# Strided attention and a gated layer on one core: 32 short filler matmuls for one of 352 columns, and a step list derived anew

## The chip, the core and the metric

The kernel runs on one core of one Trainium2 chip. The metric is the time of one execution on the device in microseconds (us), less is better; the median of several executions counts. The engines of the core work in parallel, each in its own program order: TensorE (PE, with its weight loads as PEld), VectorE (DVE), ScalarE (ACT), GpSimd (POOL) and SyncE (SP), which here issues all DMAs.

## The reference

Eight batches of eight heads with 576 positions of 64 go through attention with a mask: the first four heads see the 32 latest positions, the other four see the positions of the same residue modulo 32. The 4608 rows of 512 that come out go through a gated layer.

```python
scores = scale * np.matmul(q, k.transpose(0, 1, 3, 2))
mask_local = (rel >= 0) & (rel < stride)
mask_strided = (rel >= 0) & (pos[None, :] % stride == pos[:, None] % stride)
scores = np.where(masks[None, :, :, :], scores, -1000000000.0)
attn = np.exp(scores - max); attn = attn / (sum(attn) + 1e-09)
x = (attn @ v).transpose(0, 2, 1, 3).reshape(4608, 512)
...
gate = 1.0 / (1.0 + np.exp(-(x @ w_gate)))
out = (gate * (x @ w_val)) @ w_out
```

## The kernel before

**The work.** Attention is cut into pieces. A piece is two pairs of heads of one batch (a local one with 10 slots, 128 x 640 scores, or a strided one with 12 slots, 128 x 648). The first eight pieces (batches 0 and 1) have step names that begin with f; the others are numbered 0 to 23. Each goes through the same steps: LQ loads queries and keys, S makes the scores on PE, M adds the mask and A takes the row maximum on DVE, U subtracts it, E takes the exponential on ACT, N sums and inverts the row on DVE, W scales, B.0 to B.3 transpose 32 x 32 blocks on DVE (line 537), X multiplies with the values on PE, H and L split the result in two parts, R keeps the last columns. A score or value step is 20 to 44 small matmuls on quarters or eighths of the array.

**The gated layer.** Rows are taken in blocks of 512 (k from 0). Every operand is split into a high and a low part, so a product is three matmuls of 128x512 for each 128 of the depth. Blocks 0, 1 and 2 are done plainly: g and v (12 matmuls each), s, m, x and y on ACT and DVE, o or oh on PE. Blocks 3 to 8 are done two at a time with a seven-product scheme: G and V (lines 986, six matmuls each) make half products, c, ad, sg and mu combine them, ta to td form differences, hx and hy split the hidden values, Oa and Ob (line 1065, three matmuls each) multiply them with the output weights, ok, oa and os give out. Their weight sets are made by the kernel (steps pa, pb, ph, pw, pd), stored to device memory and read back into a ring of slots (step r).

**The order.** All of it stands in one list by hand or by an outside planner, the text ORDER. A word is a step and its numbers. The loop at the end of the kernel calls the steps in the order of the list, and every engine gets its instructions in that order; nothing is moved afterwards. A letter v or p behind a step's name (pbv, hyp, tdv, xlp) says that DVE or POOL does it in place of the usual engine.

**Fillers.** The step J issues matmuls of a constant tile whose result nobody reads. J0 makes the tile; J576, J352, J1024, J1088 and J256 (twice) stand among the first scores. They are F32 products, and the trace shows each F32 matmul as two records.

```python
    def busy(n):
        ...
        for at in range(0, n, BANK):
            m = min(BANK, n - at)
            nc.tensor.matmul(o[:, :m], ones[:, :P], ones[:, :m], start=True, stop=True)
```

The first scores (fSa0.0 and fS0.0, tiles sa and s, line 425) wait for the first load of queries and keys.

Of the kernel before, what the change touches and what calls it, by code (L numbers as in the profile page):

```python
# [96 lines left out]
wl3.1 wb4.1 wd4.1 wa5.0 ws5.0 wl3.2 wlp3.0 fg3.0 s0.3 fV1.1 wb5.1 fM1.1 y0.2 wlp2.2 wa4.2 ws4.2 wb4.2 wdp5.0 wb6.0 wu5.0 wu4.1 fg3.1 m0.3 wr6.1 x0.3
fg4.0 wl4.1 y0.3 wl5.0 wdp4.2 wr7.1 wa5.1 ws5.1 wd5.1 o0.2 wa6.0 ws6.0 wd6.0 wu4.2 wlp4.2 fg4.1 s0.4 wb6.1 wu5.1 fg5.0 wlp5.1 wu6.0 wb5.2 wr7.0 wa6.1
m0.4 x0.4 o0.3 wlp6.0 wa7.0 pl2 wb7.0 ws6.1 wd6.1 wa5.2 fg5.1 wb7.1 ws7.0 wu6.1 wd7.0 wlp6.1 ws5.2 wd5.2 s0.5 fg6.0 wu5.2 wa7.1 wl5.2 ws7.1 wd7.1 y0.4
m0.5 wu7.0 wu7.1 wa6.2 ws6.2 wb6.2 wd6.2 fg6.1 x0.5 y0.5 wlp7.1 wr8.1 wa8.1 wr7.2 s0.6 wl7.0 fg7.0 wu6.2 wl6.2 wb8.1 wb7.2 m0.6 wr8.0 wa8.0 wb8.0  # L100
ws8.0 wd8.0 wa7.2 ws7.2 wd7.2 fg7.1 fA1.1 wr8.2 fU1.1 s0.7 wu8.0 wl8.0 wr9.0 o0.4 x0.6 o0.5 wu7.2 wl7.2 y0.6 o0.6 fE1.1 ws8.1 wd8.1 wa8.2 ws8.2 fN1.1
fg8.0 wb8.2 wdp8.2 wr9.1 fWp1.1 fY1.1 wu8.1 wlp8.1 wa9.0 wb9.0 wu8.2 m0.7 fg8.1 ws9.0 wlp8.2 wr9.2 wd9.0 x0.7 wu9.0 wa9.1 fB1.1.0 fB1.1.1 fB1.1.2
wb9.1 wl9.0 wa9.2 fQ1.2 fS1.2 ws9.1 wd9.1 wr10.0 ws9.2 wb9.2 wdp9.2 wr10.1 wu9.1 y0.7 fB1.1.3 s0.8 m0.8 wa10.0 wb10.0 wu9.2 fg9.0 wlp9.1 ws10.0
wdp10.0 fg9.1 wr10.2 fM1.2 fA1.2 wb10.1 fU1.2 wa10.1 wu10.0 ws10.1 s0.9 wlp10.0 o0.7 fE1.2 fQ1.3 wlp9.2 x0.8 wa10.2 wb10.2 fX1.1 wr11.0 fV1.2 wd10.1
wu10.1 fg10.0 fn1.2 fH1.1 wr11.1 fR1.1 y0.8 ws10.2 fN1.2 fW1.2 fY1.2 wlp10.1 fB1.2.0 wdp10.2 m0.9 fg10.1 wb11.0 wa11.0 fL1.1 fS1.3 s0.10 ws11.0
wdp11.0 wu11.0 wlp11.0 wu10.2 wb11.1 wa11.1 o0.8 fg11.0 wr11.2 x0.9 pl4 fB1.2.3 fB1.2.1 fB1.2.2 fZ1.3 fM1.3 fX1.2 fV1.3 fA1.3 fU1.3 fE1.3 y0.9 m0.10
o0.9 wlp10.2 ws11.1 wdp11.1 LQ0 wu11.1 fH1.2 fR1.2 wb11.2 pl0 fN1.3 fW1.3 fY1.3 fB1.3.0 fB1.3.1 fB1.3.2 s0.11 wlp11.1 fg11.1 fB1.3.3 fL1.2 fX1.3 x0.10
y0.10 fH1.3 fL1.3 fR1.3 o0.10 pl1 g1.0 m0.11 wa11.2 ws11.2 wd11.2 x0.11 wu11.2 wl11.2 y0.11 pav0.0.0 v1.0 s1.0 m1.0 oh0.11.1 S0.0 M0.0 M0.1 oh0.11.0
pl3 A0 U0 e0.0 x1.0 y1.0 e0.1 g1.1 E0 N0 v1.1 pbv0.0.0 s1.1 g1.2 m1.1 x1.1 LQ1 LV0 v1.2 D0 y1.1 W0 d0.1 e0.3 d0.0 e0.2 Y0 B0.1 d0.3 B0.3 B0.2 o1.0
d0.2 s1.2 m1.2 S1.0 LQ2 B0.0 X0.0 po4 Z1 LV1 pa0.0.1 Y1 pb0.0.1 M1.0 M1.1 ph0.0.0.1 pwp0.0.0 pd0.0.0 R0 g1.3 v1.3 A1 U1 x1.2 y1.2 pa0.1.0 pb0.1.0 o1.1  # L110
E1 ph0.0.1.0 N1 W1 s1.3 B1.0 pw0.0.1 m1.3 x1.3 y1.3 D1 g1.4 v1.4 s1.4 g1.5 pd0.0.1 ph0.1.0.1 pav0.1.1 pbv0.1.1 ph0.1.1.0 m1.4 v1.5 pwp0.1.1 x1.4 y1.4
s1.5 pw0.1.0 o1.2 H0 L0 B1.2 B1.1 B1.3 X1.0 R1 pd0.1.1 pav1.0.1 m1.5 S2.0 M2.0 pd0.1.0 pa1.0.0 pbv1.0.0 M2.1 LQ3 A2 pbv1.0.1 ph1.0.1.0 pw1.0.1 pd1.0.1
U2 o1.3 pa1.1.1 g1.6 ph1.0.0.1 pw1.0.0 pd1.0.0 pa1.1.0 pb1.1.0 v1.6 Y2 o1.4 x1.5 y1.5 o1.5 s1.6 E2 N2 pbv1.1.1 ph1.1.1.0 pwp1.1.1 pd1.1.1 m1.6 x1.6
y1.6 ph1.1.0.1 pw1.1.0 g1.7 s1.7 H1 W2 B2.2 v1.7 m1.7 x1.7 pd1.1.0 LV2 pa2.0.0 g1.8 v1.8 o1.6 pb2.0.0 y1.7 s1.8 B2.0 L1 B2.1 B2.3 X2.0 m1.8 D2 R2 S3.0
Z3 pav2.0.1 pbv2.0.1 ph2.0.1.0 pwp2.0.1 o1.7 ph2.0.0.1 pwp2.0.0 M3.0 M3.1 po1 A3 v1.9 D3 x1.8 g1.9 LQ4 pd2.0.1 H2 Y3 U3 E3 N3 W3 pav2.1.1 y1.8 s1.9
B3.0 o1.8 B3.2 g1.10 m1.9 x1.9 LV3 y1.9 pbv2.1.1 ph2.1.1.0 pw2.1.1 B3.1 L2 pd2.0.0 B3.3 pa2.1.0 pb2.1.0 ph2.1.0.1 pwp2.1.0 s1.10 v1.10 m1.10 x1.10
# [111 lines left out]
def attention_then_glu(ctx, tc, qk_l, qk_s, v_l, v_s, w_all, consts, out, out_t):  # L228
    nc = tc.nc
# [867 lines left out]
    def by_gpsimd(step):  # L1097
# [133 lines left out]
```

## Time and profile before

| | |
|---|---|
| median of three runs | 901.21 us (899.53 to 901.92) |
| the profiled execution | 898.98 us, span 897.2 us |
| around the span | 1.78 us |
| PE busy | 889.0 us, 99% of the span |
| DVE, ACT, POOL busy | 628.8, 477.8, 327.8 us |
| instructions | 17941, of them 7050 matmuls |

The span runs from the first to the last instruction of the profiled execution. Busy times are the sum over an engine of the time in which it had an instruction. The chain that ended last is followed back from the last instruction, at each step to what released it; it tells on which engine the time was spent.

### The profile page before, as it was taken

To read this page: it belongs to the slowest core of one execution; us is meant where nothing else is said; L and a number is where in the kernel's file an instruction comes from. 1 tells how busy PE (TensorE), PEld (TensorE's weight loads), DVE (VectorE), ACT (ScalarE), POOL (GpSimd) and SP (SyncE) were. 2 spreads that over 40 slices of the span, in tenths; PEclk is the share of its full clock that TensorE was granted. 3 is DMA by queue.
4 is the path that set the end of the run, shared out by engine and by line. 5 is a ranking of instruction groups with operands and counts; after the bars stand their busy time and mean duration, and the time that the engine had idled before them with its cause. 6 is when DMAs were issued, how large, how long until landed. Compare 5 with 4: busy or idle time off the path is not lost.

```text
span 897.2 us, 17941 instructions
## 1 busy us (share of the span) xinstructions
PE 889.0 (99%) x7050; PEld 726.1 (81%) x7050; DVE 628.8 (70%) x1025; ACT 477.8 (53%) x869; POOL 327.8 (37%) x392
## 2 busy tenths in 40 slices
PE   8999999999999999999999999999999999999998
PEld 5788888888887788888878888888888888888886
DVE  6888877677778887889998976556667723433553
ACT  5888765443445554576564654344455623423453
POOL 4452631434663544675633420100132300221362
PEclk9999999999999999999999999999999999999999
DMA  9864685553573667898878758666655667655664
GB/s 349 331 229 138 217 280 168 165 163 109 158 247 99 178 182 267 245 323 288 252 249 274 258 181 271 219 205 198 216 180 194 214 192 232 195 176 204 235 205 148
DMA packets 116869, 193.63 MB, mean 216 GB/s; under 512 B 7600, under 2 KB 58800, under 8 KB 116784
## 3 DMA queue, kind: packets, MB, share of 16 engines
q1 hardware_dynamic: 116784, 192.47, 65.3%
q8 instruction: 56, 0.92, 0.4%
q14 instruction: 29, 0.24, 0.1%
HBM read 149.98 MB, written 42.47 MB: 214 GB/s over the span
## 4 chain that ended last, share of the span: by engine, by line
PE 89%; DVE 7%; ACT 2%; DMA 1%; issue 1%; SPq 0%; DVEq 0%; ACTq 0%
PE p L986 21%; PE oc L1065 19%; PE d L986 15%; PE o L713 10%; PE g L682 9%; PE v L682 9%; PE s L425 1%; PE x L603 1%; DVE pt L537 1%; PE gv L682 1%; PE x L575 1%; PE s_g L425 1%; DMA qk<-in_qk_l 1%; DVE sb L474 1%; ACT sb L489 1%
## 5 line engine op out<-in xcount | busy, mean ns | idle before, releaser
L986 PE MATMUL p<-xs,ring 128*128 128x512 f32 x864 | 210.9, 391 | 0.1
L986 PEld LDWEIGHTS p<-xs,ring 128*128 128x128 f32 x864 | 161.3, 188 | 34.2 <-issue 0.5
L986 PE MATMUL d<-xs,ring 128*128 128x512 f32 x648 | 160.0, 390 | 0.2 <-DVE hid L1013 0.2
L986 PEld LDWEIGHTS d<-xs,ring 128*128 128x128 f32 x648 | 121.2, 188 | 26.4 <-DVE hid L1013 0.9
L1065 PE MATMUL oc<-hh,ring 128*128 128x512 f32 x312 | 103.8, 389 | 0.0
L713 PE MATMUL o<-w,hh 128*128 128x512 f32 x288 | 90.5, 395 | 0.0
L1013 DVE TENSOR_TENSOR e<-e,d 128x512 f32<-128x512 f32 x54 | 37.0, 684 | 72.6 <-PE d L986 55.6
L682 PE MATMUL g<-xh,w 128*128 128x512 f32 x256 | 85.8, 393 | 0.8 <-DVE sb L449 0.5
L682 PE MATMUL v<-xh,w 128*128 128x512 f32 x256 | 85.0, 390 | 0.0
L1036 POOL TENSOR_TENSOR hid<-hid,hid 128x512 f32<-128x512 f32 x23 | 31.0, 1351 | 113.5 <-DVE hid L1030 87.8
L1065 PE MATMUL oc<-ops,ring 128*128 128x512 f32 x288 | 72.3, 389 | 0.0
L1050 ACT CAST hh<-hid 128x512 fp32r<-128x512 f32 x78 | 46.7, 620 | 42.9 <-PE oc L1065 31.5
L1065 PEld LDWEIGHTS oc<-hh,ring 128*128 128x128 f32 x312 | 58.6, 188 | 12.2
L1008 ACT COPY e<-p 128x512 f32<-128x512 f32 x54 | 31.7, 587 | 66.9 <-PE p L986 57.1
L1013 DVE TENSOR_TENSOR hid<-hid,d 128x512 f32<-128x512 f32 x54 | 36.8, 681 | 39.5 <-PE d L986 21.9
L898 POOL TENSOR_TENSOR sum<-w 128x256 f32<-128x256 f32 x49 | 39.4, 823 | 67.3 <-DMA sets<-sum 43.6
L1065 PEld LDWEIGHTS oc<-ops,ring 128*128 128x128 f32 x288 | 54.0, 188 | 11.3
L713 PEld LDWEIGHTS o<-w,hh 128*128 128x128 f32 x288 | 53.0, 188 | 11.4
L1008 ACT COPY hid<-p 128x512 f32<-128x512 f32 x54 | 31.7, 588 | 54.5 <-PE p L986 54.3
L1065 PE MATMUL oc<-hl,ring 128*128 128x512 f32 x156 | 60.7, 389 | 0.0
L903 POOL TENSOR_TENSOR sum<-sum 128x128 f32<-128x128 f32 x100 | 53.3, 534 | 18.8 <-DVE sum L898 5.5
L537 DVE STREAM_TRANSPOSE pt<-sb 32x320 f32<-32x320 f32 (+1 forms) x112 | 55.4, 495 | 3.3 <-POOL pt L376 1.0
(178 smaller groups left out, 1717.8 us busy)
## 6 DMA issues: line engine op xcount, KB each, us to landing
ring<-sets SPq DMA_DIRECT2D x126, 512.0 KB, 4.9
ring<-osets SPq DMA_DIRECT2D x63, 512.0 KB, 4.5
raw<-in_w_all SPq DMA_DIRECT2D x36, 512.0 KB, 5.7
qk<-in_qk_l SPq DMA_DIRECT2D x14, 608.0 KB, 5.0
qk<-in_qk_s SPq DMA_DIRECT2D x14, 594.0 KB, 5.4
sets<-w SPq DMA_DIRECT2D x24, 256.0 KB, 4.6
sets<-sumh SPq DMA_DIRECT2D x24, 256.0 KB, 2.9
sets<-sum SPq DMA_DIRECT2D x24, 256.0 KB, 3.1
```

The lines of the kernel that those rows point to most:

```text
L425: nc.tensor.matmul(sc[j % len(sc)][g * m : (g + 1) * m, j // len(sc) * BANK + (s - lo) * kk : j // len(sc) * BANK + (s - lo + 1) * kk], q[ ...
L537: nc.vector.transpose(dst[band * LB : (band + 1) * LB, at : at + n, col * LB : (col + 1) * LB], src[part * LB : (part + 1) * LB, x : x + n ...
L682: nc.tensor.matmul(o, w, x, start=first and n == 0, stop=last and n == len(todo) - 1)
L713: nc.tensor.matmul(acc[k][i], h[:, i * P : (i + 1) * P], w, start=f == 0 and n == 0, stop=f == NF - 1 and n == 2,)
L898: by.tensor_tensor(to, part(wh[f][i], c), part(wl[f][i], c), op=ALU.add)
L903: by.tensor_tensor(u[:, to], u[:, x], u[:, y], op=op)
L986: nc.tensor.matmul(to, w[:, (wi * 2 + c) * P : (wi * 2 + c + 1) * P], x[xi][:, c], start=p in (1, 2, 5) and c == j == 0, stop=c == 1 and j ...
L1008: nc.scalar.copy(x, two[m, 0])
L1013: nc.vector.tensor_tensor(x, x, two[m, 1], op=ALU.add)
L1036: by.tensor_tensor(h[to], h[x], h[y], op=ALU.subtract)
L1050: nc.scalar.copy(ops[q, p][0], hidden_tile(k, q, KEPT[str(p)]))
L1065: nc.tensor.matmul(chains[m, at], w[:, (wi * 2 + m) * P : (wi * 2 + m + 1) * P], x[xi], start=p in (1, 2, 5) and q == j == 0, stop=q == PA ...
```

## The change

The step J352 becomes Jt32: 32 matmuls of 32 columns with 32 columns of weights, all of the same constant tile and to the same place. From its eighth line on the list has its steps in a new order; they are the same steps, but 74 of them are given to the other one of DVE and POOL (among them sum parts pb, differences ta to td, low parts hy and xl). The values of piece 20 (X20.1) and the scores of piece 21 (S21.1) stand behind each other in it.

```diff
-fQb0.0 fZ0.0 fZ0.1 J0 K fZ0.3 fZ0.2 fQa0.0 fQa0.1 fQb0.1 wr2.0 fQ0.2 wr1.0 fQ0.3 C J576 fK0.1 wr0.0 fV0.1 fKa0.0 fV0.0 fK0.0 fV0.2 J352 fSa0.0 fV0.3
+fQb0.0 fZ0.0 fZ0.1 J0 K fZ0.3 fZ0.2 fQa0.0 fQa0.1 fQb0.1 wr2.0 fQ0.2 wr1.0 fQ0.3 C J576 fK0.1 wr0.0 fV0.1 fKa0.0 fV0.0 fK0.0 fV0.2 Jt32 fSa0.0 fV0.3
...
+    def busy_short(n):
+        ones, o = busy_with
+        for _ in range(n):
+            nc.tensor.matmul(o[:32, :32], ones[:, :32], ones[:, :32], start=True, stop=True)
+
...
     STEPS = dict(
-        J=busy,
+        J=busy, Jt=busy_short,
...
-Oa3.4.4 Ob3.4.4 B20.2 Oa3.5.4 Ob3.5.4 r57 S21.1 os3.1.7 ok3.0.4 ok3.1.4 V5.0.1 G5.0.1 r58 c5.0.1.1 oa3.0.3 G5.0.2 os3.0.3 c5.0.0.1 os3.1.4 V5.0.6
-c5.0.1.6 ad5.0.0.2 V5.0.2 G5.0.6 r59 ad5.0.1.2 V5.0.5 sg5.0.2 mu5.0.2 G5.0.5 c5.0.0.6 B20.1 hx5.0.1 B20.3 Z21 M21.0 R19 xh5.1.3 xlp5.1.3 M21.1 A21
-G5.0.7 c5.0.0.7 ad5.0.0.7 U21 V5.0.7 c5.0.1.7 G5.0.4 ad5.0.1.7 V5.0.4 r60 sg5.0.7 mu5.0.7 E21 sg5.0.4 X20.1 os3.0.7 H20 Y21 N21 V5.0.3 G5.0.3 LQ22 r63
...
+hyp3.4.4 Ob3.4.4 Oa3.4.4 r54 B20.2 R19 Ob3.5.4 B20.1 B20.3 X20.1 S21.1 LQ22 Oa3.5.4 ok3.1.4 V5.0.1 ok3.0.4 G5.0.1 c5.0.0.1 r56 V5.0.2 oa3.0.3 G5.0.2
```

On PE, at the program's beginning, unread is the fillers' place, s and sa are the first scores; this is one piece of the difference:

```order
 L412 LDWEIGHTS cst
 L412 MATMUL s_0_130<-cst 128x128
-L802 MATMUL unread<-ones 128x352
+L807 MATMUL unread<-ones 32x32 x32
 L425 MATMUL sa_0_125<-qk_0_80 32x64 x24
 L425 MATMUL s_0_130<-qk_0_80 32x64 x12
 L425 MATMUL s_1_118<-qk_1_100 64x54 x22
```

The filler keeps its place, between the last mask products and the first scores, which stand behind it in PE's queue.

On PE, between the last output products of blocks 3 and 4 (oc3) and the first half products of blocks 5 and 6 (p15), the scores of piece 21 (s21) stood alone before:

```order
L1065 MATMUL oc3_1_1_5994<-hh3_5_4_6535,ring52_6460 128x512
L1065 MATMUL oc3_1_1_5994<-hl3_5_4_6536,ring52_6460 128x512
L1065 MATMUL oc3_1_1_5994<-hh3_5_4_6535,ring52_6460 128x512
L425 MATMUL s21_6571<-qk7_1_6245 64x54 x24
L986 MATMUL p15_0_6601<-xs5_1_0_5834,ring53_6508 128x512
```

The values of piece 20 (x20) followed 72 matmuls of 128x512 later. Now both stand together, three matmuls ahead of the end of oc3:

```order
L1070 MATMUL oc3_1_1_6019<-hh3_5_4_6563,ring52_6468 128x512
L1070 MATMUL oc3_1_1_6019<-hl3_5_4_6564,ring52_6468 128x512
L1070 MATMUL oc3_1_1_6019<-hh3_5_4_6563,ring52_6468 128x512
L575 MATMUL x20_6601<-pt7_0_6505,vv7_0_6188 64x96 x2
L575 MATMUL x20_6601<-pt7_0_6505,vv7_0_6188 64x64 x2
L575 MATMUL x20_6601<-pt7_0_6505,vv7_0_6188 64x96 x12
L575 MATMUL x20_6601<-pt7_0_6505,vv7_0_6188 64x64 x2
L575 MATMUL x20_6601<-pt7_0_6505,vv7_0_6188 64x32 x2
L425 MATMUL s21_6622<-qk7_1_6387 64x54 x24
L1070 MATMUL oc3_0_1_6025<-hh3_5_4_6563,ring52_6468 128x512
```

So x20 stands 75 matmuls of 128x512 earlier than before, and s21 three earlier.

On DVE at the same place, the normalisation (mx7_0, sb7_0) and the transposes (pt7_0, line 537) of piece 20, which x20 reads, before:

```order
L1081 TENSOR_TENSOR ot3_1_6_6297<-ot3_1_6_6297,oc3_1_5_6293 128x512
L1054 TENSOR_TENSOR ops3_5560<-hid3_5_4974,ops3_5560 128x512
L1054 TENSOR_TENSOR ops3_5560<-hid3_8_5353,ops3_5560 128x512
L1054 TENSOR_TENSOR hl3_5_4_6536<-hid3_13_5893,hh3_5_4_6535 128x512
L1054 TENSOR_TENSOR hl3_4_4_6498<-hid3_10_5602,hh3_4_4_6497 128x512
L495 TENSOR_REDUCE mx7_0_6203<-sb7_0_6202 128x10
L504 TENSOR_SCALAR mx7_0_6203<-mx7_0_6203 128x10
L505 RECIPROCAL mx7_0_6203<-mx7_0_6203 128x10
L513 TENSOR_TENSOR sb7_0_6202<-sb7_0_6202,mx7_0_6203 128x640
L537 STREAM_TRANSPOSE pt7_0_6430<-sb7_0_6202 32x9x32
L537 STREAM_TRANSPOSE pt7_0_6430<-sb7_0_6202 32x10x32 x3
L1081 TENSOR_TENSOR ot3_0_6_6291<-ot3_0_6_6291,oc3_0_5_6305 128x512
```

The other four transposes stood behind three sums of the next blocks. Now:

```order
L1086 TENSOR_TENSOR ot3_1_5_6450<-ot3_1_5_6450,oc3_1_1_6019 128x512
L495 TENSOR_REDUCE mx7_0_6232<-sb7_0_6231 128x10
L504 TENSOR_SCALAR mx7_0_6232<-mx7_0_6232 128x10
L505 RECIPROCAL mx7_0_6232<-mx7_0_6232 128x10
L1086 TENSOR_TENSOR ot3_1_6_6321<-ot3_1_6_6321,oc3_1_5_6326 128x512
L1059 TENSOR_TENSOR ops3_5589<-hid3_8_5388,ops3_5589 128x512
L513 TENSOR_TENSOR sb7_0_6231<-sb7_0_6231,mx7_0_6232 128x640
L537 STREAM_TRANSPOSE pt7_0_6505<-sb7_0_6231 32x9x32
L537 STREAM_TRANSPOSE pt7_0_6505<-sb7_0_6231 32x10x32 x6
L537 STREAM_TRANSPOSE pt7_0_6505<-sb7_0_6231 32x9x32
L1086 TENSOR_TENSOR ot3_0_6_6316<-ot3_0_6_6316,oc3_0_5_6339 128x512
```

All eight transposes stand together, and behind the sum ot3_1_6 there is one low part (ops3) ahead of them where there were four; the other three are POOL's now.

## Rows read from the trace of the kernel before

**Rows 1.** The page: busy engines with their share, and the chain that ended last.

```profile
PE 889.0 (99%) x7050; PEld 726.1 (81%) x7050; DVE 628.8 (70%) x1025; ACT 477.8 (53%) x869; POOL 327.8 (37%) x392
PE 89%; DVE 7%; ACT 2%; DMA 1%; issue 1%; SPq 0%; DVEq 0%; ACTq 0%
```

**Rows 2.** PE's waits over the whole span: total us, times, longest us.

```profile
PE unread L802 <- POOL ones L796: 1.5, 1, 1.5
PE x L603 <- issue: 0.8, 2, 0.5
PE g L682 <- DVE sb L449: 0.5, 1, 0.5
...
PE d L986 <- DVE hid L1013: 0.2, 1, 0.2
```

**Rows 3.** Windows, 350 to 500 us: PE, PEld, DVE, ACT, POOL busy (count).

```profile
350.00:500.00 150.00, 149.70 (x1321) 122.07 (x1320) 133.14 (x215) 90.64 (x163) 81.39 (x105) 1.00 0.82 269
```

**Rows 4.** The chain that ended last, 0 to 46 us: start us, us, what.

```profile
1.65 4.80 DMA qk<-in_qk_l
...
6.49 0.68 PE sa L425 x41
...
7.27 0.62 DVE mx L463 x2
...
10.09 0.57 ACT words L301
...
22.97 1.42 PE x L603 x72
```

**Rows 5.** Three windows, fillers alone: length, PE busy (records), PEld busy, granted clock.

```profile
1.40:3.30 1.90, 1.78 (x2) 0.84 (x3) 1.00 0.64 180
4.70:6.30 1.60, 1.49 (x2) 0.53 (x2) 1.00 0.98 373
8.90:10.90 2.00, 1.88 (x4) 0.64 (x4) 1.00 1.05 421
```

**Rows 6.** PE's filler in the timeline; then PE groups by shape, 0 to 26 us.

```profile
4.78 1.49 PE L802 MATMUL unread<-ones 128*128 128x352 f32 x2
...
L425 PE MATMUL sa<-qk 64*32 64x64 f32 x48 | 0.7, 225 | 0.2 <-DMA qk<-in_qk_l 0.2
L425 PE MATMUL s<-q 64*32 64x64 f32 x48 | 0.7, 223 | 0.0
```

**Rows 7.** The chain again, 541 to 566 us and 614 to 624 us.

```profile
540.82 2.72 PE oc L1065 x12
543.54 0.85 PE s L425 x48
544.39 2.94 PE p L986 x12
...
560.93 0.92 PE x L575 x36
561.86 2.95 PE d L986 x12
...
618.51 0.86 PE x L575 x34
619.37 0.75 PE s L425 x48
620.12 1.59 PE p L986 x6
```

**Rows 8.** DVE's timeline, 535 to 556 us: start us, us, what, idle before it.

```profile
535.42 0.69 DVE L1081 TENSOR_TENSOR ot<-ot,oc 128x512 f32<-128x512 f32 x1 [2.32 <-PE oc L1065]
...
540.31 0.82 DVE L513 TENSOR_TENSOR sb<-sb,mx 128x640 f32<-128x640 f32 x1
541.17 2.02 DVE L537 STREAM_TRANSPOSE pt<-sb 32x288 f32<-32x288 f32 x4
...
553.38 2.06 DVE L537 STREAM_TRANSPOSE pt<-sb 32x320 f32<-32x320 f32 x4
```

More of the change, by code (lines that the diff above doesn't have):

```diff
@@ L97 @@
[L97 to L116, printed above, removed]
@@ new lines @@
+xl5.0.4 xdv5.1.1 Oa3.0.5 hx3.5.5 Oa3.1.5 Oa3.2.5 hx3.0.7 Ob3.2.5 xh5.1.6 hx3.1.7 Oa3.3.5 hy3.0.7 Ob3.0.7 Ob3.3.5 hy3.4.5 Oa3.4.5 Ob3.4.5 hy3.5.5
+Ob3.5.5 xl5.1.6 xdv5.1.3 xh5.1.5 r47 xl5.1.5 xh5.1.4 hy3.1.7 LQ21 Oa3.0.7 td3.4 hx3.2.7 hx3.3.7 Oa3.1.7 xd5.1.2 xh5.1.7 Oa3.5.5 hx3.4.7 r48 hy3.2.7
+hy3.3.7 Ob3.1.7 hx3.0.3 Ob3.2.7 os3.1.2 Ob3.3.7 tdv3.3 hx3.5.7 hy3.4.7 hy3.0.3 Oa3.2.7 D20 xl5.1.4 ok3.0.5 Oa3.3.7 hx3.1.3 hx3.2.3 r50 hyp3.1.3
+xl5.1.7 ok3.1.5 Oa3.4.7 hy3.5.7 r49 Ob3.4.7 Ob3.5.7 Oa3.5.7 r52 Ob3.0.3 hy3.2.3 Oa3.0.3 Oa3.1.3 Ob3.1.3 r53 oa3.0.7 hx3.5.3 Ob3.2.3 Oa3.2.3 hx3.3.3
@@ new lines @@
+mu5.4.3 V5.5.2 r85 tb5.2 hy5.4.1 tc5.3 G5.5.2 r88 c5.5.0.1 G5.5.6 X23.1 xh7.1.1 c5.5.1.1 V5.5.6 ad5.5.1.2 V5.5.5 xh7.0.2 ad5.5.0.2 H23 r86 c5.5.0.6
+G5.5.7 xlp7.0.2 tav5.4 c5.5.1.6 V5.5.7 r90 G5.5.5 xh7.1.2 xl7.1.2 mu5.4.7 c5.5.0.7 r89 ad5.5.0.7 tc5.4 xh7.0.1 c5.5.1.7 ad5.5.1.7 G5.5.4 G5.5.3
+sg5.5.4 sg5.5.7 tbv5.4 V5.5.4 V5.5.3 sg5.5.2 ad5.5.0.3 sg5.5.3 mu5.5.7 Oa5.0.1 Oa5.1.1 Oa5.2.1 R23 z r91 xh7.1.3 mu5.5.4 ad5.5.1.3 mu5.5.3 Oa5.3.1
+mu5.5.2 tav5.5 tb5.3 Ob5.0.1 hx5.5.1 Ob5.1.1 r93 Ob5.2.1 hy5.5.1 Ob5.3.1 xlp7.1.1 xlp7.1.3 Oa5.4.1 hx5.0.2 hy5.0.2 hx5.1.2 hx5.2.2 hy5.1.2 Oa5.5.1
@@ new lines @@
+ok5.0.6 Oa5.2.5 xl7.0.5 hx5.3.5 hy5.3.5 Ob5.1.5 Ob5.2.5 Ob5.3.5 hx5.4.5 xdv7.0.2 xh7.0.7 xl7.0.7 ok5.1.6 Oa5.3.5 os5.0.2 hyp5.4.5 Oa5.4.5 Ob5.4.5
+hx5.5.5 hx5.1.7 hy5.5.5 Ob5.5.5 hx5.0.7 xdv7.1.0 xdv7.1.1 hy5.0.7 r101 Ob5.0.7 xh7.1.5 Oa5.5.5 hx5.3.7 xl7.1.5 xdv7.1.2 hx5.2.7 Oa5.0.7 hx5.5.7
+hy5.1.7 Oa5.1.7 xh7.1.6 tdv5.1 hy5.2.7 hy5.3.7 Ob5.1.7 Ob5.2.7 Oa5.2.7 xh7.0.3 xl7.1.6 Oa5.3.7 hx5.4.7 xdv7.1.3 xh7.1.4 xh7.1.7 hy5.4.7 Ob5.3.7
+Ob5.4.7 hy5.5.7 Ob5.5.7 r100 xl7.1.4 Oa5.4.7 hx5.0.3 hx5.1.3 hy5.0.3 hy5.1.3 ok5.0.5 Oa5.0.3 Oa5.1.3 hx5.2.3 xl7.1.7 ok5.1.5 Oa5.5.7 r102 hx5.3.3
@@ new lines @@
+Ob5.0.3 Ob5.1.3 hyp5.3.3 hy5.2.3 Oa5.2.3 hx5.0.4 Ob5.2.3 hx5.4.3 hx5.1.4 Oa5.3.3 oa5.1.7 oa5.0.7 r103 r105 hy5.0.4 Ob5.0.4 Oa5.0.4 hx5.5.3 hy5.4.3
+Oa5.4.3 td5.2 hyp5.1.4 Ob5.3.3 hx5.2.4 Ob5.4.3 r104 hy5.5.3 Oa5.5.3 Ob5.5.3 hy5.2.4 td5.3 hx5.3.4 r106 hx5.4.4 Oa5.1.4 Ob5.1.4 r108 Ob5.2.4 hy5.3.4
+Ob5.3.4 td5.5 hx5.5.4 hyp5.5.4 Oa5.2.4 Oa5.3.4 hy5.4.4 Oa5.4.4 os5.1.2 Oa5.5.4 ok5.0.4 Ob5.4.4 Ob5.5.4 ok5.1.4 oa5.0.3 G7.0.2 xl7.0.1 G7.0.1 V7.0.1
+oa5.1.3 V7.0.2 c7.0.0.1 os5.1.7 ad7.0.0.2 G7.0.5 r107 c7.0.1.1 ad7.0.1.2 V7.0.5 r109 G7.0.6 c7.0.0.6 r113 V7.0.6 c7.0.1.6 r110 G7.0.7 c7.0.0.7
@@ new lines @@
+os7.1.2 hy7.0.3 hx7.1.3 hx7.2.3 Ob7.4.7 Ob7.5.7 oa7.1.7 Oa7.4.7 hx7.3.3 Oa7.5.7 oa7.0.7 hx7.4.3 r157 tdv7.2 os7.0.7 Oa7.0.3 hyp7.1.3 Oa7.1.3 hyp7.2.3
+Oa7.2.3 Ob7.0.3 Ob7.1.3 hx7.0.4 hy7.0.4 Ob7.2.3 hx7.1.4 hyp7.3.3 tdv7.4 Oa7.3.3 Ob7.3.3 Ob7.0.4 Oa7.0.4 hx7.5.3 hy7.5.3 hyp7.4.3 Ob7.4.3 hx7.2.4
+hy7.2.4 Oa7.4.3 os7.1.7 Oa7.5.3 Ob7.5.3 oa7.1.3 hyp7.1.4 Ob7.1.4 Oa7.1.4 r156 Oa7.2.4 hx7.5.4 hyp7.5.4 oa7.0.3 os7.0.3 hx7.4.4 td7.3 Ob7.2.4 os7.1.3
+hx7.3.4 hy7.3.4 Ob7.3.4 Oa7.3.4 hy7.4.4 Oa7.4.4 Oa7.5.4 ok7.0.4 Ob7.4.4 Ob7.5.4 os7.0.4 ok7.1.4 os7.1.4
```

208 lines of the change are left out of this document (105 added, 103 removed).

## The prediction

> **What bounds the kernel now.** I read the page first: PE is busy for 889.0 of 897.2 us and holds 89% of the chain that ended last [rows 1]. The waits of PE say how little it stands still: the first is the making of the filler tile, and the eight groups of the list together are 4.0 us, of which the 2.3 us behind the first scores come in pieces of 0.5 us or less [rows 2]. The chain prices the stream itself: 12 matmuls of 128x512 in 2.72 us, 0.2267 us each [rows 7]. The list holds 3564 of them before and after, 808 us, so nine tenths of the time can't move. What can move is the first 22 us, where the chain goes over DMA, PE, DVE and ACT in turn [rows 4], the gaps where the stream goes over to small matmuls and back [rows 7], and stalls.
>
> **The filler.** Up to 4.78 us all is as before. The old filler begins there and takes 1.49 us [rows 6], to 6.27; the load that the first scores wait for lands at 6.45, and they begin at 6.49 [rows 4]. So the old filler cost nothing: the load hid it, with 0.2 us to spare. The new one has 64 records (two for each F32 matmul), and no row shows a record of this shape. The clock decides what they take. The page's granted clock reads 1.00 in all three windows, but the records tell two levels: two passes of 512 columns take 1.78 us near the start and four take 1.88 us at 8.9 us [rows 5], 1.74 and 0.92 ns a column, 1.2 and 2.4 GHz. The old filler's two passes of 352 columns still ran at the low level (1.49 us, 2.1 ns a column [rows 5]). The first scores, behind it, ran at the high one: 225 ns a record as against 223 for equal ones at 11 us [rows 6]. So the clock rose between 6.27 and 6.49 us, after PE had worked from 1.5 us on nearly without a break.
>
> At these rates 32 columns are 0.056 us low and 0.029 us high. If the clock rises at about 6.5 as before, 31 records are done by then ((6.5 - 4.78) / 0.056), and the other 33 take 0.97: the filler ends at 7.47 and the first scores begin 1.0 us late. The ends: records of small matmuls spread over the array follow each other in 0.017 us (41 in 0.68) to 0.020 (72 of 32 columns in 1.42) [rows 4]; 64 at 0.017 end at 5.87, ahead of the load, and cost 0. All 64 at the low level take 3.6 us, end at 8.34 and cost 1.85. I take 1.0, nearer to the filler's own rows, because the new matmuls all go to the same 32 columns of the array and can't lie beside each other as those small ones do. At 0.020 and its double it would be 0.4.
>
> Does a late start stay? The chain goes from the first scores (6.49) to the row maximum on DVE (7.27), over ACT, where the conversion of the first weights stands in line (10.09), to the products at 22 us [rows 4]. No later piece of it in this stretch is a DMA, so nothing waits there for something that doesn't move too. Queued behind the filler on PE are the first scores, and behind those the other pieces' scores and J1024; for them DVE, then ACT, wait. From 23 us on PE has no wait to give it back to. I count the whole 1.0.
>
> The Trainium skill has a figure that bears on this (TensorE: Matmul & The Clock Gate, section "Wait — 56ns, not 53.3ns?"): start to start never falls below some 25 ns, however short a matmul. The small records here follow in 17 ns across the array [rows 4], so there the trace differs; for one place of the array no run here shows it. By the page 64 records are at least 1.6 us, which ends at 6.4 and would cost nothing.
>
> **The joined run.** Alone, the scores of 21 take 0.85 us, and the first 12 matmuls behind them 2.94 in place of 2.72; the values of 20 take 0.92 and the 12 behind them 2.95 [rows 7]. Sum 0.85 + 0.22 + 0.92 + 0.23 = 2.22. The same pair of shapes in one run (values and scores at 618.5): 0.86 + 0.75, and 1.59 in place of 1.36 for the six behind, 1.84 [rows 7]. The joined run saves 0.38 us. All other runs of small matmuls stay as they were, joined or alone (38 runs before, 37 now, counted along PE's order), so this is the whole of it.
>
> It adds a condition: x20 comes 75 matmuls earlier, at about 542.8 us of the old time, and reads all eight transposes. Before, four ended at 543.2 and four at 555.4 [rows 8]. Now: the sum that waits for PE's chain starts at 535.42 as before and ends near 536.1; one low part (0.6), the scaling (0.82) and twice the 2.02 us of four transposes [rows 8] end at 541.6. That is 1.2 us early, two DVE instructions of 0.6. I price it at 0; if three more stand ahead, the stall is 0.6 us, and all that PE has queued waits with it.
>
> **The rest of the list.** On PE only neighbours change places, by 24 matmuls at most apart from x20. Loads of the ring: counted along PE's order, the shortest way from the last use of a slot to the first use of what is then loaded there is 30 matmuls (6.8 us) in both lists. The moves between DVE and POOL take work from the fuller engine (DVE 133 of 150 us at 350 to 500, POOL 81 [rows 3]) to the emptier. I take 0, with 2.3 us either way as bounds: all of the old small waits gone, or as much again.
>
> **Sum.** Against the profiled execution: span 897.2 + 1.0 - 0.38 = 897.8, and 1.78 around it, 899.6 for its 898.98. The median of the runs, 901.21, lies 2.2 above that execution, so the forecast for a median is 901.21 + 0.6 = **901.8 us**. A measurement of this kernel can tell about 0.3%, 2.7 us, from no change; this is within it.
>
> **Rivals.**
> - *The filler stays hidden.* It ends before 6.45, as the small records of [rows 4] would; only the joined run counts: 901.21 - 0.38 = 900.8. Against it: one place of the array for all 64. Chance 0.23.
> - *The clock rises later (slower).* The old filler had the whole array at work until just before the rise; 32 columns are a quarter of it. If that doesn't count as before, all 64 records go at the low level (1.85), the first scores (0.68) take double (0.7), and the small products and products on the way to 22 us too for as long as it lasts: with the fillers at 9 us doubled (0.9) that is 3.4, 901.21 + 3.4 - 0.38 = 904.2. For it: nothing in the rows says what the chip wants; against it: PE is then busier in time than before, without the 0.2 us gap. It decides from 3.1 us lost at the start on. Chance 0.13. The Trainium skill says (same page, section "What's actually happening") that the low clock is the default and activity releases it; the trace agrees, low at 1.4 us and high at 8.9 [rows 5].
> - *New stalls.* A list derived anew can wait where the old one did not, most easily at 350 to 500 us where DVE is full to 89% [rows 3], or at x20. Doubling the old waits gives 901.8 + 2.3 = 904.1. PE's longest wait there was 0.2 us [rows 2], which speaks against it. Chance 0.12.
> - *The stalls go.* The old waits vanish, and the filler costs nothing or 1.0: 901.21 - 0.38 - 2.3 = 898.5 to 899.5. Chance 0.09.
>
> The forecast keeps 0.43. **Range:** 899.2 to 904.5; its own, from the filler's ends, is 900.8 to 902.7. Faster by over 0.3% needs the last rival at its best: 0.04. Slower by over 0.3% (above 903.9) takes two thirds of the late clock and a third of the new stalls, 0.09 + 0.04 = 0.13. The rest, 0.83, is the same.
>
> **What would show it.** The profile after should have the first sa record near 7.5 us in place of 6.49, 64 filler records spaced 0.056 and then 0.029 us, the long stream beginning 1.0 us later; near 543.7 one run of values and scores with one slow start behind it, and no wait at its head; PE's waits still some 2 us in small pieces. The first scores at 6.5 us would make the filler hidden; scores with records of twice the spacing, the late clock. A PE wait of over 1 us anywhere behind 25 us makes the forecast wrong by a stall, and its releaser's line names the step.

## The result and the profile after

The changed kernel takes 908.4 us (median of 6 executions, 904.3 to 910.4) against 899.5 for the kernel before, measured beside it (median of 6, 898.6 to 901.9): 1.0082 of its time, 95% interval 1.0064 to 1.0101 (this ratio comes from all executions; the quotient of the two medians is 1.0099). The forecast was 901.8 in 899.2 to 904.5. The profiled execution is the shortest, 904.26 us, its span 902.5.

First the page of the changed kernel: the busy engines, the chain by engine, and the queue that brings instructions (packets, MB, share).

```profile
PE 891.9 (99%) x7112; PEld 730.9 (81%) x7112; DVE 624.4 (69%) x1004; ACT 481.0 (53%) x871; POOL 345.3 (38%) x413
PE 91%; DVE 3%; DMA 3%; POOL 1%; issue 1%; ACT 1%; SPq 0%; DVEq 0%; POOLq 0%
q8 instruction: 56, 0.92, 0.4%
```

PE has 62 matmuls and 62 weight loads more than in [rows 1]. Next the waits of PE over the whole span, as in [rows 2].

```profile
PE s L425 <- issue: 1.8, 2, 1.5
PE unread L802 <- POOL ones L796: 1.5, 1, 1.5
PE x L603 <- issue: 0.9, 1, 0.9
PE p L991 <- DMA ring<-sets: 0.7, 2, 0.5
...
PE d L991 <- DMA ring<-sets: 0.5, 1, 0.5
```

The two largest new ones have no releaser: "issue" is time in which the profile shows nothing that PE waited for. The chain from 5 to 28 us says where they stand (start us, us, what); it answers to [rows 4].

```profile
4.99 3.23 PE unread L807 x64
8.22 0.59 PE sa L425 x41
...
12.84 0.36 PE s L425 x25
13.19 1.49 issue
14.68 0.71 PE s L425 x45
...
25.46 0.58 PE x L603 x16
26.05 0.94 issue
26.98 1.22 PE x L603 x55
```

Both lie in the middle of a run of small matmuls, the scores and the values of early pieces. The first scores begin at 8.15 in place of 6.49. Behind the second wait the clock fell to 1.2 GHz for 3.4 us: windows 24:27 and 27:30 (length, the busy time of PE, PEld, DVE, ACT and POOL, then the granted clock, the DMA share and GB/s).

```profile
24.00:27.00 3.00, 1.71 (x21) 0.93 (x22) 2.82 (x5) 2.19 (x5) 1.56 (x2) 1.00 1.03 406
27.00:30.00 3.00, 3.00 (x61) 2.56 (x61) 1.10 (x2) 1.71 (x4) 0.00 (x0) 0.68 1.01 404
```

By the 36th of the 3564 large matmuls (35.8 us before) the changed kernel is 4.70 us late; its whole profiled execution is 5.3 longer than the profiled one before. The joined run came as forecast, here in the chain at 548 us, and its first value has no wait ahead of it:

```profile
548.00 0.86 PE x L575 x34
548.86 0.75 PE s L425 x48
```

**What PE waited for.** The packets of the queue q8 answer it. One lies in the window 12.1 to 13.3 us, none in 9 to 12.1 or in 13.3 to 18.3, and the DMA engines are full (their share of the data alone is 99.6%). The queues in that window (packets, MB, share):

```profile
q1 hardware_dynamic: 153, 0.48, 99.6%
q8 instruction: 1, 0.02, 5.6%
```

A packet is 16384 bytes (0.92 MB in 56). All that the traces show of PE counts here, in order: weight loads, matmuls and the few semaphore instructions between them. In the first 33 us PE's waits without a releaser stand at the 449th, 705th, 961st and 1217th instruction, always 256 apart: 1.49, none, 0.94 and 0.28 us in the changed kernel, none, 0.27, 0.21 and 0.51 in the kernel before. Such a place, where one packet's instructions end, is called a border below, and the 256 instructions between two of them a block. This table is worked out from the packets and the instructions in the traces (us):

```
block starts at      449            705            961            1217
                  landed goes on  landed goes on  landed goes on  landed goes on
kernel before     12.12  14.24    18.22  19.72    24.30  25.80    30.53  32.06
changed kernel              13.23      14.68      19.45      21.00      25.44   26.98    31.57  33.04
```

Apart from the first one of the kernel before, where PE had work of its own until 14.2, PE goes on some 1.5 us after a packet has landed, in both kernels (at the 705th of the changed kernel without a wait, since its own work ended just then). From 14.7 to 33 us the changed kernel enters three blocks in 18.4 us, 6.1 for each or 24 ns for an instruction; the kernel before is not much quicker (17.8 from 14.2 us), though it waits only 1.0 us there in all. So **in this stretch PE is held by the supply of its instructions**, in the kernel before only just. As an estimate, 124 instructions more are 124 x 24 ns = 3.0 us more. The Trainium skill describes the machinery (Runtime: NRT & Kernel Launch, section "Instruction fetch mechanics"): instructions come in blocks of 16 KiB, 256 of them, over a DMA queue of the sequencer's own, and crossing a border is mostly hidden. The trace agrees on the blocks; here the crossing was not hidden.

### The profile page after: what moved, and what is told of

It reads as the page before. It is cut to its first block, busy times and chain, and to the rows that moved or that the text cites. A ratio compares the mean times of both kernels' runs of the same rounds, so it can differ in the third digit from the quotient of the medians.

```text
span 902.5 us, 18077 instructions
## 1 busy us (share of the span) xinstructions
PE 891.9 (99%) x7112; PEld 730.9 (81%) x7112; DVE 624.4 (69%) x1004; ACT 481.0 (53%) x871; POOL 345.3 (38%) x413
## 4 chain that ended last, share of the span: by engine, by line
PE 91%; DVE 3%; DMA 3%; POOL 1%; issue 1%; ACT 1%; SPq 0%; DVEq 0%; POOLq 0%
PE p L991 20%; PE oc L1070 19%; PE d L991 16%; PE o L713 9%; PE g L682 9%; PE v L682 9%; DMA ring<-sets 2%; PE s L425 2%; PE x L603 1%; PE unread L802 1%; DVE pt L537 1%; PE gv L682 1%; PE x L575 1%; PE s_g L425 1%; POOL sum L908 1%
## 5 line engine op out<-in xcount | busy, mean ns | idle before, releaser
L908 POOL TENSOR_TENSOR sum<-sum 128x128 f32<-128x128 f32 x124 | 66.2, 534 | 22.6 <-DVE sum L903 11.1
L903 POOL TENSOR_TENSOR sum<-w 128x256 f32<-128x256 f32 x50 | 41.9, 858 | 61.7 <-DMA sets<-sum 22.6
L1059 POOL TENSOR_TENSOR hl<-hid,hh 128x512 fp32r<-128x512 f32 x26 | 37.1, 1430 | 54.6 <-ACT hh L1055 54.4
L682 PEld LDWEIGHTS g<-xh,w 128*128 128x128 f32 x256 | 48.3, 189 | 11.0 <-DVE sb L449 0.7
```

Of the source, the lines that this page charges most:

```text
L682: nc.tensor.matmul(o, w, x, start=first and n == 0, stop=last and n == len(todo) - 1)
L903: by.tensor_tensor(to, part(wh[f][i], c), part(wl[f][i], c), op=ALU.add)
L908: by.tensor_tensor(u[:, to], u[:, x], u[:, y], op=op)
L1059: by.tensor_tensor(hl, hidden_tile(k, q, KEPT[str(p)]), hh.bitcast(F32), op=ALU.subtract)
```

## The experiments

Fillers are named by the columns (J352: 352 columns) or by the number of short matmuls (Jt32: 32). Ratios are to the kernel before, measured beside each run; the runs of e, f, g and h were on four different chips, so runs of different letters are best compared by their ratios. The ranges that I had expected stand in the quotations.

```
                      list filler J256s  other            us   ratio  interval
changed kernel        new  Jt32                       908.40  1.0082  1.0064-1.0101
e1_list               new  J352                       902.96  1.0034  1.0016-1.0052
e2_filler             old  Jt32                       904.80  1.0061  1.0041-1.0081
e3_wide_late          new  J1376                      908.28  1.0094  1.0057-1.0130
e4_short_hidden       new  Jt14          J512 Jt18    907.52  1.0076  1.0046-1.0106
f1_double             new  Jt32          J512 Jt18    909.26  1.0099  1.0081-1.0116
f2_fewer              old  J352   none   no J1088     900.65  1.0005  0.9991-1.0019
f3_after_again        new  Jt32                       907.50  1.0070  1.0036-1.0105
f4_list_again         new  J352                       902.21  1.0017  1.0004-1.0031
g1_old_wide_late      old  J1376                      900.55  1.0017  0.9999-1.0034
g2_old_short_hidden   old  Jt14          J512 Jt18    906.21  1.0058  1.0038-1.0078
g3_old_joined         old  J352          x20 moved    901.16  1.0010  0.9996-1.0024
g4_old_longer_fillers old  J352   J512                899.65  0.9992  0.9979-1.0005
h1_after_longer       new  Jt32   J512                907.53  1.0072  1.0050-1.0093
h2_list_longer        new  J352   J512                903.09  1.0028  1.0010-1.0046
h3_old_short_half     old  Jt16   J512                903.31  1.0025  1.0011-1.0038
h4_old_short_longer   old  Jt32   J512                903.69  1.0035  1.0020-1.0050
```

How much later than before the k-th large matmul begins in each profile (us, from the traces; "clock" is where the granted clock stood at one half behind 9 us):

```
k (time before)         36 (35.8) 1500 (405) 1750 (472) 2300 (604)       last   clock
changed kernel               4.70       4.42       5.49       5.29       5.27   28-31
f3_after_again               3.95       6.48       7.71      11.94      11.94   26-33, 603-606
e1_list                      3.30       4.44       7.16       6.52       6.57   21-31
e2_filler                    4.41       3.80       3.30       4.83       4.83   25-32
e3_wide_late                 1.14       1.46       7.00       6.34       6.35   451-454
e4_short_hidden              3.47       4.70       5.32       9.28       9.29   27-30, 600-604
f1_double                    9.70      10.33      11.48      10.85      11.14   21-24, 31-38
f2_fewer                     3.15       2.82       2.71       2.51       2.51   15-32
f4_list_again                1.66       3.44       7.07       6.41       6.41   451-454
g1_old_wide_late             1.03       0.64       0.60       0.25       0.94   none
g2_old_short_hidden          4.76       5.28       5.71       7.61       7.61   15-18, 28-32
g3_old_joined                0.56       0.46       0.94       2.28       2.28   none
g4_old_longer_fillers        0.35       1.57       1.07       0.72       0.72   none
h1_after_longer              4.41       5.23       5.51       9.00       9.00   33-36, 599-603
h2_list_longer              -0.29       0.63       1.44       0.76       0.75   none
h3_old_short_half            3.75       4.79       4.88       4.54       6.07   27-31
h4_old_short_longer          3.87       3.59       3.19       4.73       4.73   none
```

**The parts of the change, one by one.** e1_list is the new list with the old filler, e2_filler the old list with the new filler:

```diff
-fV0.2 Jt32 fSa0.0
+fV0.2 J352 fSa0.0
```

> The new list with the old filler of 352 columns in its place. If the filler carries the loss (its length, its 124 more instructions on PE, or the clock behind it), this run is near the kernel before: 899.1 to 900.1 us, the joined run at 543 giving 0.4 back and the new waits on loads at 419, 452 and 569 us taking up to 1.0. If the new order carries the loss, it is 903 or more, and the waits sit behind 100 us.

> The old list with the 32 short matmuls. If the filler carries the loss: 906 to 909 us, with the first scores at 8.15 us, PE standing still without a releaser in the scores near 13 us and in the values near 26 us, and a granted clock of one half for some us behind that. If the order carries it: 900 to 901.5 (the late start of 1.7 at most).

The two halves make up the whole: 0.34% and 0.61%, together 0.95 beside 0.82, each good to about 0.2%. So the filler is probably the larger part, and the list is not free: e1_list's 902.96 lies at the edge of what I had given for the new order (903 or more), and e2_filler's 904.80 under what I had given for the filler alone (906 to 909). In e2_filler PE waits without a releaser in the scores (1.3 us at 13 us) and in the values (1.2 at 26 us), as expected. In e1_list the waits on loads that I expected were not there; one large wait stood in the chain at 449 us, again without a releaser:

```profile
446.10 1.03 PE s L425 x61
447.13 0.92 PE x L575 x35
448.05 1.35 PE p L991 x5
449.41 2.99 issue
452.40 0.50 PE p L991
```

It is at PE's instruction 9153 = 449 + 34 x 256, a border of blocks; the packet landed at 450.95, 1.45 us before PE went on. The 96 small matmuls of one joined run take 1.95 us, so the block ran out before the next came, and the DMA engines were busy meanwhile. Windows of e1_list, then of the kernel before, where the same border fell at 444.9 us and cost PE nearly nothing:

```profile
446.00:448.00 2.00, 1.99 (x122) 1.77 (x121) 1.90 (x4) 1.98 (x3) 0.00 (x0) 1.00 0.87 261
448.00:450.00 2.00, 1.41 (x7) 0.84 (x5) 1.79 (x4) 1.99 (x5) 0.42 (x1) 1.00 0.97 340
```

```profile
440.00:442.00 2.00, 2.00 (x46) 1.45 (x48) 1.90 (x4) 1.97 (x3) 0.07 (x1) 1.00 1.01 371
442.00:444.00 2.00, 2.00 (x99) 1.79 (x89) 2.00 (x4) 1.43 (x4) 0.85 (x1) 1.00 0.27 102
```

In the old list the DMA engines are full too until 442, but then fall to 0.27, and the packet begins 1.7 us after PE has entered the block ahead; in the new list they stay at 0.87 to 0.97, and it begins 4.8 us after. That the loads delay the packet is argued from this alone: no run changes the loads and nothing else. The same new list once more was to tell chance from cause.

> The new list with the old filler once more. If the 3.0 us that PE stood still at 449 us come from the new list (loads that keep the DMA engines busy while the block of instructions is fetched): a stall of 2 to 4 us at the same matmul again. If that was chance: 0.5 or less.

It waited 2.3 us at the same instruction. In e3_wide_late it was 3.5 and in h2_list_longer 1.1; in the four profiles of the old list with the border there (the kernel before, g1_old_wide_late, g3_old_joined, g4_old_longer_fillers) it was 0.8 or less. This profile also has a wait of another kind, at 376 us, for DVE, which was late itself: its sums stood behind a store of weight sums that took 6.7 us (two of the profile's waits, then that store in its chain):

```profile
PE p L991 <- issue: 2.3, 1, 2.3
PE d L991 <- DVE hid L1018: 1.5, 1, 1.5
```

```profile
367.69 6.70 DMA osets<-sum
```

No profile of the old list has this wait.

**Late start or number of instructions.** e3_wide_late and g1_old_wide_late start the first scores late with few instructions; e4_short_hidden and g2_old_short_hidden have nearly all the instructions (120 more than before in place of 124) and start in time. The edits for the new list; in the old one the same words take the place of J352 and J1024:

```diff
-fV0.2 Jt32 fSa0.0
+fV0.2 J1376 fSa0.0
```

```diff
-fV0.2 Jt32 fSa0.0
+fV0.2 Jt14 fSa0.0
...
-fE0.1 J1024
+fE0.1 J512 Jt18
```

> The new list with a filler of 1376 columns in place of the 32 short ones: about as long (to 8.2 us) but 12 instructions on PE in place of 128. If only the late start costs and all else follows from it: as the changed kernel, 907 to 909 us, stalls and clock fall included. If the number of instructions makes PE wait for its next block of them: the first scores come 1.7 us late as well, but PE does not stand still near 13 and 26 us, the clock stays at 1.00 between 24 and 45 us, and the time is the one of the new list with the old filler plus 1.7, some 901 to 902.

> The new list with 14 short matmuls in place of the 32 (over at about 6.4 us, before the load that the first scores wait for), and 18 more short ones in place of the second half of the filler of 1024 columns at 9 us: the same number of PE instructions by 11 us as in the changed kernel, but no late start. If the late start is what costs: 899 to 900.5 us. If the supply of instructions is: the first scores at 6.5 us, and PE still stands still without a releaser 1.5 us or more in the scores at 11 to 14 us and about 1 us in the values near 25 us, the long stream begins 2.5 us or more later than at 45.0, and the time is 902 to 908.

> The old list with a filler of 1376 columns in place of the 352: the late start of the first scores without the extra instructions, and without anything of the new list. If the number of PE instructions carries the loss of the short filler: 899.5 + 1.1 = 900.6 us (the 36th big matmul 1.1 us later, as with the new list), against 904.8 for the 32 short matmuls in the old list. If the late start carries it: 904 to 905.

> The old list with 14 short matmuls ahead of the first scores (hidden by the load) and 18 behind in place of half of the filler of 1024: as many PE instructions as with 32, and the first scores on time. If the number of PE instructions carries the loss: 903 to 905 us, the 36th big matmul 3 to 4 us later than before. If the late start carries it: 899.5 to 900.

In the old list the answer is plain: 900.55 for the late start alone (its first scores stand at 7.66 us), 906.21 for the instructions alone. The supply explains the second, but it is above the 903 to 905 that I expected of it; the clock was at one half for 6.8 us of its start. PE's first scores and waits in g2_old_short_hidden (start and length; then total, times, longest):

```profile
6.56 0.95 PE L425 MATMUL sa<-qk 64*32 64x64 f32 x47
```

```profile
PE s L425 <- issue: 3.9, 3, 2.0
```

With the new list e4_short_hidden agrees (first scores at 6.51, 907.52), and so does the start of e3_wide_late: 1.14 us at the 36th matmul, no wait without a releaser ahead of it, the clock full up to 450 us. But its median, 908.3, is 6 us above what I expected of the supply, and lies in the 907 to 909 that I had given for the late start. Of the lateness, 4.7 us came in its profile at 446 us, from the border above and the clock behind it. Six executions spread from 902 to 913, and what makes this one so much worse than e1_list stays open. So by the time it is the old list alone in which the instructions are told from the late start; with the new list only the start of the profiles tells them apart.

**More instructions, and fewer.**

```diff
-fE0.1 J1024
+fE0.1 J512 Jt18
```

> The changed kernel with 18 more short matmuls in place of the second half of the filler of 1024 columns at 10 us: 68 more PE instructions, none of them ahead of the first scores. If PE is held by the supply of its instructions in the first 33 us (256 of them per 6.1 us, so 24 ns for each): the first scores at 8.15 us as in the changed kernel, but the stretch from there to the 36th big matmul (at 40.5 us there) ends 1.6 us later, near 42; the same blocks of instructions are entered at the same times, with less of the program in them; time 909.5 to 912. If the late start is what costs: 908.4 again, and 40.5.

f1_double's 909.26 is just under the range that I gave for the supply. The blocks were entered at 13.9, 20.3 and 28.2 us, and its waits lie in whatever PE does at a border, here in a filler itself:

```profile
PE s L425 <- issue: 2.0, 1, 2.0
...
PE unread L807 <- issue: 1.4, 1, 1.4
PE x L603 <- issue: 1.3, 1, 1.3
```

The start lost 9.7 us in place of 6.3, with the clock at one half for 10 us of it, as against 3.4 in the changed kernel; half of those 6.8 us more, an estimate of what they cost, is 3.4. The third block was entered 1.2 us later than in the changed kernel and not at the same time. So the start lost more, as the supply has it, but the price of an instruction can't be read here, and the whole time can't be told from the changed kernel's (the intervals overlap). The other direction:

```diff
-fA0.2 fWp0.1 wr3.1 fU0.2 J1088 fS0.3
+fA0.2 fWp0.1 wr3.1 fU0.2 fS0.3
...
-ws0.0 J256 fT0.0
+ws0.0 fT0.0
...
-fW0.2 J256 fX0.1
+fW0.2 fX0.1
```

> The kernel before without the fillers of 1088, 256 and 256 columns at 12, 15.4 and 16.6 us: 20 fewer PE instructions. If the supply binds up to 33 us also in the kernel before: the 36th big matmul at 35.3 in place of 35.76 us, and the time 0.3 to 0.8 lower, 898.7 to 899.2. If the supply only hurts the changed kernel, or if the fillers keep the clock up: 899.5 or more, in the second case with a granted clock of one half between 14 and 30 us.

No gain: without these fillers the clock fell at 14.7 us and stayed down for 17 us. Windows 14:17 and 17:20 of f2_fewer, and 14:17 of g4_old_longer_fillers, in which these two fillers are longer:

```profile
14.00:17.00 3.00, 2.98 (x32) 2.35 (x32) 2.83 (x7) 2.54 (x5) 1.82 (x3) 0.62 1.05 423
17.00:20.00 3.00, 2.75 (x88) 2.75 (x92) 3.00 (x4) 3.00 (x12) 3.00 (x3) 0.50 1.02 397
```

```profile
14.00:17.00 3.00, 3.00 (x57) 2.20 (x56) 2.71 (x7) 1.99 (x4) 2.11 (x2) 1.00 1.02 412
```

So f2_fewer says nothing on the supply; it shows what these fillers are worth.

**The clock.**

```diff
-ws0.0 J256 fT0.0
+ws0.0 J512 fT0.0
...
-fW0.2 J256 fX0.1
+fW0.2 J512 fX0.1
```

> The old list with 512 columns in each of the two fillers of 256: no instruction more, 0.6 us more of PE's work between 15 and 17 us. If PE is held by the supply of instructions there, the two fill time that PE would stand: the 36th big matmul at 35.8 us as before. If PE's own work binds there: 36.4. If low activity is what lets the clock fall at 20 to 32 us: fewer executions with a granted clock below 1.00 (11 of 25 before), and a median 0.5 to 1 us lower, 898.5 to 899; if not, 899.5 to 900.

> The changed kernel with 512 columns in each of the two later fillers of 256: in the old list that kept the granted clock at full speed in 12 of 12 executions. If the clock's falls are a part of the changed kernel's loss: 905.5 to 906.5 us, and a mean clock of 0.999 or 1.000 in most executions. If they only come with the loss: 907.5 to 908.5.

> The new list with the old filler of 352 and the two later fillers at 512 columns. The clock held, what is left against the old list with the same fillers (899.65) is the new list alone. If it loses by the stall at 449 us (2.3 to 3.0 in two profiles): 901 to 902, with the stall there again. If it lost by the clock: 899.2 to 900.

> The old list with 32 short matmuls and the two later fillers at 512. If the clock is the smaller part: 904.8 - 1.5 = 903.3 us, so 3.7 above the old list with the same fillers (124 instructions at 24 ns and 1.0 of late start, less the overlap of the two). If the clock is most of the filler's loss: 900 to 901.

The edit is the same in the four: in the old list, in the changed kernel, in the new list with J352, and in the old list with Jt32. In the old list the mean granted clock was 0.999 or more in all 12 executions of g4_old_longer_fillers, as against 20 of 30 of the kernel before, measured beside it, and 0.6 us more of PE's work cost 0.35 us at the 36th matmul. The time, 899.65, can't be told from before. In the changed kernel the longer fillers did not hold the clock (0.993 to 0.998, 907.53): there it falls behind the waits for instructions, and what the clock alone is worth there isn't told by this run. The Trainium skill has the low clock as the default that activity releases (TensorE: Matmul & The Clock Gate, section "What's actually happening"). The rows agree at 450 and 600 us, where each fall in these profiles begins 2 to 5 us behind the start of a wait for instructions, of 2.3 to 3.5 us (one of 3.0, in e1_list, has no fall behind it); at 20 to 32 us it fell in e1_list with no such wait ahead.

Against the common 899.65 the parts stand by themselves: the short filler 903.69 - 899.65 = 4.0 us, the new list 903.09 - 899.65 = 3.4, the sum 907.1, both together 907.53. The 899.65 is of another chip; by the ratios of the table the parts are 3.9 and 3.2 us, each good to about 2, and both together 7.2. The wait at 449 us was only 1.1 in the profile of h2_list_longer, which is of its shortest execution (899.7, of 899.7 to 905.6), so the 3.4 are not all seen in rows. h4_old_short_longer shows the filler's part without any fall of the clock: its first scores come at 8.10 us, but its 1217th instruction is entered at 32.21, 0.15 later than before, so the late start is gone by then. What is left, 3.87 - 0.15 = 3.7 us at the 36th matmul, is the 124 instructions, 30 ns each (28 against g4_old_longer_fillers, which is 0.35 late itself).

**A second profile of the changed kernel.**

> The changed kernel once more, for a second profile. If its loss is the supply at the start: the 36th big matmul is again 4 to 5 us later than before, plus a quarter of whatever time the clock is at one half; the other waits change from run to run by 1 to 3 us.

This execution (span 909.1) shows what the first profile had not. The start lost 3.95, less than I expected (4 to 5, and a quarter of the 6.8 us for which the clock was at one half). At 599 us it stood at instruction 11457 = 449 + 43 x 256, and the clock fell behind the wait; the chain, then two windows:

```profile
597.72 0.84 PE x L603 x44
598.56 0.88 PE s L425 x56
599.44 3.05 issue
602.49 0.42 PE s L425 x10
```

```profile
599.00:602.00 3.00, 0.44 (x37) 0.28 (x26) 1.20 (x2) 1.38 (x2) 0.35 (x2) 1.00 0.73 272
602.00:605.00 3.00, 2.52 (x15) 1.96 (x16) 1.91 (x3) 0.00 (x0) 0.00 (x0) 0.60 0.38 110
```

The 124 instructions move every later border by as many places. This one lies in a joined run of 110 small matmuls in all seven profiles with 120 or 124 more; six of these waited there, 1.6 to 3.05 us (the seventh is the first profile of the changed kernel), and none of the nine with the old number, some 8 more or 20 fewer did. In the seventh its packet had landed at 592.5, before PE had even entered the block ahead. Another 2.7 us of the second profile's lateness arose between 384 and 411 us, its large matmuls 1400 to 1500. There PE waited for a load of the ring (0.9 us) and for ACT and DVE (1.0), not for instructions.

**Half the instructions.**

```diff
-fV0.2 J352 fSa0.0
+fV0.2 Jt16 fSa0.0
```

> The old list with 16 short matmuls in place of the 352 (60 PE instructions more, the first scores at most 0.1 us late) and the two later fillers at 512. If each PE instruction before 33 us costs 24 ns: 899.65 + 1.4 = 901.1 us, the 36th big matmul 1.4 to 1.8 us later than before, plus up to 1.5 of stalls where the blocks' borders now fall. If the price has a threshold near 124: 899.7.

There is no threshold: 60 instructions cost 3.75 us at the 36th matmul (with the clock at one half for 3.4 us) and 3.7 in the median. Its waits at the start, 1.4 in the scores and 1.0 in the values, are almost those of 124. By the medians the price isn't linear. But 11 of the 12 executions have a mean clock below 1.000, and the only other one took 901.71, 2.1 us above 899.65; of 124 instructions the two executions at 1.000 took 902.11 and 903.70. Whether the price is linear where the clock holds isn't shown.

**The joined run alone.** In the old list the values of 20 and what they need are taken from their places and stand ahead of the scores of 21:

```diff
-r57 S21.1 os3.1.7
+r57 R19 B20.1 B20.3 X20.1 S21.1 os3.1.7
```

> The old list with one thing of the new: the values of 20 (with the two transposes and the multiplication that they need) stand ahead of the scores of 21. If the joined run works as in the changed kernel: 0.4 us less behind 545 us and no wait at its head, 899.1 us, which a measurement can't tell from 899.5. If the values come too early for DVE: a wait of up to 0.6 us at their head, 899.5 to 900.

It waits at its head for DVE's transposes, the worse of the two cases and by more than its bound of 0.6; between the 2035th and the 2170th large matmul (539 and 572 us before) it loses 1.3 us:

```profile
PE x L575 <- DVE pt L537: 0.8, 1, 0.8
```

## Why the prediction was wrong

- **The filler's time: right.** The records of 32 columns follow in 0.053 us at the low clock and 0.032 at the high one, for a forecast of 0.056 and 0.029. When the clock rose differs from execution to execution, so the 64 took 3.30 us in the first profile, 2.34 in the second and 2.21 in e2_filler; the first scores were 0.6 to 1.7 us late, around the term of 1.0 and inside its bounds. The filler in the timeline of the first profile and of the second (start, length):

```profile
4.92 3.30 PE L807 MATMUL unread<-ones 128*32 128x32 f32 x64
```

```profile
4.92 2.34 PE L807 MATMUL unread<-ones 128*32 128x32 f32 x64
```

- **"I count the whole 1.0": right for a late start alone** (g1_old_wide_late, 1.03 us at the 36th matmul, though only 0.6 are left at 405 us), but beside 124 instructions it is absorbed (h4_old_short_longer).
- **What failed is the step that priced the filler by the time of its records alone.** It had no term for what PE must be sent: 128 instructions in place of 4, at a place where PE gets 256 per 6.1 us. That term is 3.0 us at this rate and 3.7 measured at the 36th matmul (h4_old_short_longer). The sign stood in [rows 2]: the waits "x L603 <- issue" in the middle of a run of small matmuls were taken as small pieces of stall, when they stood where the supply had just begun to hold PE. The sign that the prediction named for a stall, a PE wait of over 1 us behind 25 us, just missed in the first profile: 0.94 us at 26 us, the larger one at 13. The sum forecast 0.6 us more than before, and the medians differ by 8.9. Its base, 901.21, was itself 1.7 above the later median of six.
- **"The rest of the list: 0, with 2.3 either way" failed as well.** The new list costs 3.4 us with the longer fillers (1.5 to 3 in the other two). Of the mechanism, the wait at the border at 449 us is shown, 1.1 to 3.5 us in four profiles, and the busier DMA engines beside it; the wait for DVE at 376 us was in one of them. How much of the 3.4 each is worth stays open. The old small waits did go and come in part, as the bounds had it; they were not what decided. The rival of new stalls had the stretch, 350 to 500 us, but not the releaser.
- **The joined run: right**, and that x20 has time as well; only in company of the rest of the list, as g3_old_joined shows. Between the 2035th and the 2170th large matmul eight of the nine profiles with the new list gain 0.29 to 0.33 us on the kernel before, for a forecast of 0.38. The ninth, the first profile of the changed kernel, loses 0.15 there.
- **"The clock rises later"** wasn't it. It rose at 7.6 us in the first profile and at 5.3 in the second, around the 6.5 of the forecast, and fell afterwards, for which the forecast had no case.
- The price changes from execution to execution: 6.7 us lie between the two profiles of the changed kernel, most of it from the border at 599 us with the clock behind it and from 384 to 411 us.

Open: what exactly makes the clock fall at 20 to 32 us also where no wait stands ahead of it (e1_list); the price of an instruction, 28 to 62 ns in the runs (falls of the clock included); the median of e3_wide_late, and with it what a late start is worth under the new list. No version beat the kernel before by more than a measurement can tell.

## What to carry to other kernels

Count instructions where small matmuls stand close together and the DMA engines are full: there this filler's price was the number of its instructions, and the same time on PE is bought with a few wide ones (in the old list 1376 columns in 12 instructions cost 1 us at the start, 32 short matmuls in 128 cost 4). A PE wait "issue" inside a run of independent matmuls is the sign; see whether such waits are a multiple of 256 instructions apart, semaphore instructions counted too, and whether a packet of the instruction queue landed just before PE went on. And instructions added early move every later border, so a change at 5 us can make a stall at 600.

## What the hardware showed unexpectedly

- Every wait of PE without a releaser of 0.2 us or more, 47 in the eighteen profiles, stands at a border, a multiple of 256 instructions behind the 449th. PE went on 1.2 to 1.6 us after the block's packet had landed. At the start the packet began 2.9 to 3.9 us after PE had entered the block ahead of it (the kernel before and the first profile of the changed one); at 449 us of e1_list, with the DMA engines at 0.87 to 0.97, 4.8 us; at the same border of the kernel before, with 0.27 in the window in which it began, 1.7. So no packet had come far ahead of its use at these places, and a run of small matmuls could use up a block before the next one came.
- A wait of 3 us for instructions can cost half as much again: in the second profile of the changed kernel the clock fell to 1.2 GHz for 3.4 us behind it (0.60 in the window at 602 us), which is an estimated 1.7 us, half of that time.
- Short matmuls all on the same 32 columns of the array follow each other in 0.032 us at 2.4 GHz; those spread over it in 0.017 [rows 4].
